# Seven products instead of eight for the last two chunks in layer 0 too, with the sums that feed them moved

## The chip, the core and the metric

The kernel runs on one NeuronCore of one Trainium2 chip. The metric is the device time of one execution in microseconds (us), lower is better. Names in the profile: PE is TensorE (matmuls), PEld its weight loads, DVE is VectorE, ACT is ScalarE, POOL is GpSimd, SP is the engine whose queue issues most DMAs. A q behind an engine's name (SPq, ACTq) is its queue issuing a DMA.

## The reference

Two layers, each an attention block and a gated MLP block, on an x of 2048 rows and 512 columns, with the same weights in both layers, all in float32:

```python
def _A_ref(x, wqkv, wo):            # linear attention, 32 heads of 16
    q, k, v = ...(x @ wqkv)
    phi = lambda t: jnp.where(t > 0, t + 1, jnp.exp(t)) + 1e-6
    kv = einsum("bhsd,bhse->bhde", phi(k), v);  z = sum of phi(k) over s
    o = (phi(q) @ kv) / (phi(q) @ z + 1e-6)
    return o.reshape(B, S, D) @ wo

def _B_ref(x, w_in, w_sp, b_sp, w_out):   # F = 1792, half of it 896
    z = _gelu(einsum("bsd,df->bsf", x, w_in))
    z1, z2 = z[..., :Fh], _layernorm(z[..., Fh:])
    g = einsum("ts,bsf->btf", w_sp, z2) + b_sp[None, :, None]
    return einsum("bsf,fd->bsd", z1 * g, w_out)

x = x + _A_ref(_layernorm(x));  x = x + _B_ref(_layernorm(x))   # twice
```

## The kernel before, in words

**Arithmetic.** Every float32 operand of a matmul is split into a high part (a copy on ScalarE, rounded to the matmul's type, `high`, L101) and a low part (the rest, a subtraction on VectorE, `low`, L104). A product is then three matmuls: high by high, high by low, low by high (`mm3`, L115 to L117). So each operand costs one ScalarE and one VectorE operation, and each 128 x 512 result over 512 columns of x costs 12 matmuls.

**Order of the work.** Nothing is scheduled by a planner: the order of the Python code is the order in which each engine gets its instructions, and each engine works through its own list in order. Waits between engines come from the tiles that they share. SBUF tiles come from lists of slots (`Slots`, L30): 22 pages of 128 x 512, 6 quads of 128 x 4 x 512, 4 larger ones; a slot that was freed first is reused first, and a DMA into it waits for its last reader.

**Stages of a layer.** x is cut into 16 tiles of 128 rows (four chunks of four tiles).

- `P1`, steps s = 1 to 17: layer norm, turning of the tile (`T`), K and Q projections, phi, and the sum G over the tiles (`Gmm(s-2)`). `start` (L416) opens it in layer 0: first loads, warm-up matmuls that compute nothing (`idle`), first tile and weights.
- `transition`: from G to the matrix that replaces attention's kv and wo.
- `P2`, steps s = 1 to 18 (`run`, L888). In step s: `c(s-1)`, attention's output of a tile, with the residual add `c2` and statistics `c_stats` (VectorE, then three small operations on GpSimd); `c3(s-1)`, normalise on ScalarE, and store the tile (yt) for turning; `b(s)` and `d(s-2)`, where a loaded tile is transposed by VectorE (L286) and split; `e(s-3)`, the half of w_in that becomes z2 (24 matmuls), with gelu `e2` and statistics `e3`; `e4(s-4)`, its normalisation; and then up to two units `f` of the other half, z1: one unit is one of 7 feature blocks of one of 4 chunks, 12 matmuls and a gelu.
- `P4`, 56 groups and then 16 tiles `o`: the spatial product with w_sp (already done with seven block products instead of eight, so it needs sums of w_sp's blocks: `Sums`, whose `tick` does two adds on GpSimd, its fetches and its stores, in P2 and P4 of layer 0), gates, and the out-projection. `join` starts the next layer's P1 beside the tiles `o`.

**Seven products.** In layer 1 alone (`self.seven`), feature blocks 0 to 5 of the chunks 2 and 3 are not computed as 12 units `f`. They are seen as a 2 x 2 block product: 3 blocks of features against 3 others, 256 columns of x against the other 256, chunk 2 against chunk 3. Seven products of 6 matmuls per block (`product`, L776) then take the place of eight. They need four sums of blocks of w_in and four sums of blocks of x:

- The weight sums are made once, by `Make` (L165): `fetch`, `add` (four operations on VectorE), `split`, `store` into a DRAM buffer, in steps beside the tiles `o` at the end of layer 0 (`make.step(i)`, L1249). In layer 1 `fetch_sum` (L769) loads them from GpSimd's queue.
- The x sums are made tile by tile of chunk 3. `whole` (L739) adds high and low part of the matching tile of chunk 2 on GpSimd, in steps 13 to 16; `block_sums` (L745) does four 256-wide subtractions on VectorE, inside `d_low` (L672); `block_parts` (L761) splits a finished half.
- The products P1 and P2 lie in the steps 14 to 16 (`side`, L861), P3 to P7 in `tail` (L821), behind step 18. The unit 6 of each chunk remains (`last_f`).

In layer 0 the units f of the chunks 2 and 3 go on until they are done, the last of them behind step 18 (`P4.run`, L1205).

Of the kernel before, what the change touches and what calls it, by code (L numbers as in the profile page):

```python
# [53 lines left out]
def mixer_kernel(ctx: ExitStack, tc: tile.TileContext, x_in, wqkv, wo_d, win1_d, win2_d, wsp_d, bsp_d, wout_d,  # L54
# [109 lines left out]

    class Make:  # L165


        def __init__(self):
            self.raw, self.sum, self.part = {}, {}, {}

        def fetch(self, g):
            self.raw[g] = load(win1_d[g]), load(win1_d[g + 3])

        def add(self, g):
            a, b = self.raw.pop(g)
            A11, A12, A21, A22 = (r.rearrange("p (c f) -> p c f", f=P)[:, s] for r in (a, b) for s in (slice(0, 2), slice(2, 4)))
            s, t = pages.get([P, 2, 2, P]), pages.get([P, 2, 2, P])
            nc.vector.tensor_add(s[:, 0], A21, A22)
            nc.vector.tensor_sub(s[:, 1], s[:, 0], A11)
            nc.vector.tensor_sub(t[:, 0], A11, A21)  # L180
            nc.vector.tensor_sub(t[:, 1], A12, s[:, 1])
            pages.put(a, b)
            self.sum[g] = s, t

        def split(self, g):
            self.part[g] = []
            for r in self.sum.pop(g):
                h, l = pages.get([P, 2, 2, P], F32R), pages.get([P, 2, 2, P], F32R)
                split(h, l, r)
                pages.put(r)  # L190
                self.part[g] += [h, l]

        def store(self, g):
            for n, p in enumerate(self.part.pop(g)):
                m = 2 * (n // 2)
                nc.sync.dma_start(kept[:, m:m + 2, g, n % 2, :], p.bitcast(F32).rearrange("p m c f -> p m (c f)"))
                pages.put(p)

        def step(self, i):
            for g in range(3):  # L200
                at = i - 2 * g
                if 0 <= at < 5:
                    (self.fetch, lambda g: None, self.add, self.split, self.store)[at](g)
# [87 lines left out]
    class P1:  # L291
# [124 lines left out]
        def start(self):  # L416
# [19 lines left out]
            idle(10)  # L436
# [3 lines left out]
            self.wk.piece()  # L440
            self.T_high(0)
            idle(4)
# [3 lines left out]
            self.wk.piece()  # L446
# [9 lines left out]
        def run(self):  # L456
# [5 lines left out]
            for s in range(1, NT + 2):  # L462
                self.loadx(s + 3)
                self.turn.load(s + 1)
                turned = 2 <= s < NT and s not in self.turn.by_pe
# [31 lines left out]
                for w in list(side)[:1 if s < 5 else 2]:  # L497
                    w.fetch()

# [69 lines left out]
    class P2:  # L569
        def __init__(self, p1):  # L570
            self.L = L = p1.L
            self.p1 = p1
            self.win1, self.win2 = w_in1(), p1.win2
            self.qturn, self.xturn = Turn(f"qt{L}", range(5), True), Turn(f"yt{L}", range(4))
            self.qp, self.qT, self.x, self.ms, self.xB, self.z, self.zms = {}, {}, {}, {}, {}, {}, {}
            self.fq = deque()
            self.fnext = []
            self.seven = self.L == 1
            self.S, self.T, self.Tp = {}, {}, {}
# [92 lines left out]
        def d_low(self, i):  # L672
            b, home, h, l = self.dpart
            low(l, b, h)
            n, k = divmod(i, 4)
            if self.seven and n == 3:
                self.block_sums(k, b)
            home.put(b)
            if i in self.xB:
                pages.put(self.xB.pop(i))  # L680
            if k == 3 and not (self.seven and n >= 2):
                self.fnext = [(n, f) for f in range(NF)]
# [30 lines left out]
        def f(self):  # L713
# [8 lines left out]
            if f == NF - 1 and not (self.seven and n == 3):  # L722
                quads.put(*self.xT.pop(n))
# [15 lines left out]
        def whole(self, k):  # L739

            h, l = (t[:, :, k * P:(k + 1) * P].bitcast(F32) for t in self.xT[2])
            self.xr = pages.get([P, 4, P])
            nc.gpsimd.tensor_tensor(self.xr, h, l, op=OP.add)

        def block_sums(self, k, y):  # L745


            p, o = divmod(k, 2)
# [4 lines left out]
            x = self.xr  # L753
# [5 lines left out]
            pages.put(x)  # L759
# [9 lines left out]
        def fetch_sum(self, m):  # L769
            self.S[m] = []  # L770
            for g in range(3):
                t = pages.get([P, 2, 2, P], F32R)
                nc.gpsimd.dma_start(t.rearrange("p i c f -> p i (c f)"), kept[:, m - 1, g])
                self.S[m].append(t)
# [27 lines left out]
        def P1(self, g):  # L802
            if g == 0:
                self.X, self.C = [], []
            self.X.append(banks.get(PAGE))
            self.product(self.X[g], "P1", g, start=True)
            self.C.append(self.copied(self.X[g]))

        def P2(self, g):
            y = banks.get(PAGE)  # L810
            self.product(y, "P2", g, start=True, stop=True)
            t = self.C[g]
# [4 lines left out]
        def last_f(self, n):  # L817
            self.fq.append((n, NF - 1))
            self.f()

        def tail(self, p4):  # L821
            self.last_f(3)
# [38 lines left out]
        def side(self, s):  # L861

            if s == 14:
                self.P1(0)
                self.P1(1)
            elif s == 15:
                self.P1(2)
                self.P2(0)
                self.fetch_sum(4)
            elif s == 16:  # L870
                self.P2(1)
                self.P2(2)
                self.fetch_sum(2)
                for m in (2, 3):
                    self.block_parts(m, 0)
            elif s == 17:
                self.last_f(2)
                self.block_parts(2, 1)
                self.block_parts(3, 1)
                self.fetch_sum(3)  # L880
            elif s == 18:
                for m in (4, 1):
                    for p in range(2):
                        self.block_parts(m, p)
            if 13 <= s < 17:
                self.whole(s - 13)

        def run(self, sums):  # L888
            w1 = self.win1
            for s in range(1, NT + 3):  # L890
# [16 lines left out]
                else:  # L907
# [32 lines left out]
                if self.seven:  # L940
                    self.side(s)
# [4 lines left out]
                if s > 7:  # L946
                    sums.tick()
                if s >= NT + 1 and not self.seven:
                    self.p4.fetch(s - NT - 1)
# [4 lines left out]
    class Sums:  # L954
# [26 lines left out]
        def tick(self):  # L981
# [3 lines left out]
            if not self.raw:  # L985
                self.fetch()
            self.fetch()
# [13 lines left out]
    class P4:  # L1001
# [189 lines left out]
        def o(self, i):  # L1191
# [6 lines left out]
            nc.vector.tensor_add(x, x, b)  # L1198
            banks.put(b)
            nc.sync.dma_start(xs[2 * self.L + 2, i], x)  # L1200
# [4 lines left out]
        def run(self, nxt):  # L1205
            p2 = self.p2
            if p2.seven:
                p2.tail(self)
            else:
                self.prepare(0, 0)  # L1210
                self.fetch(2)
                while p2.f():
                    pass
                p2.win1.free()
                self.prepare(1, 1)
                self.fetch(3)
                self.prepare(None, 2)
            self.gb = [bigs.get([P, NF, 512]) for _ in range(NCHK)]
            n = len(self.steps)
            for g in range(n):  # L1220
# [4 lines left out]
                if g in (1, 4, 7) or 8 <= g < 28:  # L1225
# [16 lines left out]
            make = Make() if nxt is not None else None  # L1242
            for i in range(NT):
                self.loadx(i + 2)
                self.gates()
                self.o(i)
                self.zsplit(i + 2)
                if make is not None:
                    make.step(i)  # L1249
# [3 lines left out]
        def join(self, i, nxt):  # L1253
# [16 lines left out]
            if i == 15:  # L1270
                nxt.T(1)

    sums = Sums()
    p1 = P1(0)
# [43 lines left out]
```

## Time and profile before

| what | value |
|---|---|
| median of 3 runs | 1393.94 us (1392.9 to 1395.38) |
| the profiled execution | 1392.76 us |
| its span, first to last instruction | 1391.0 us |
| TensorE busy | 1383.0 us, 99% of the span, 6252 instructions |
| VectorE busy | 908.8 us, 65% |
| ScalarE, GpSimd busy | 595.1 us, 43%; 429.2 us, 31% |
| DMA | 233.57 MB, mean 168 GB/s |
| P2 of layer 0, of layer 1 | about 139 to 332 us, 829 to 1016 us |
| granted TensorE clock | 1.000 over the span |

The page gives busy time per engine, the span in 40 slices, the chain of work that ended last (followed back from the last instruction to what released each step), and the costliest groups. The views of the trace give the instructions of an engine in order of time with their start, length, source line, operation and tiles; behind them in brackets stands how long the engine was idle just before, and what released it. Matmuls are pipelined: one of 128 x 512 lasts 0.39 us in the record, but the next starts about 0.23 us later, and this distance is what it costs.

### The profile page before, as it was taken

How to read it: one execution, taken by the hardware profiler on the slowest of the kernel's cores; microseconds unless marked ns; L12 is line 12 of the kernel's file. 1: busy time of each engine (PE TensorE's matmuls, PEld its weight loads, DVE VectorE, ACT ScalarE, POOL GpSimd, SP SyncE). 2: the span in 40 equal slices, each digit the busy share in tenths (PEclk: the TensorE clock that was granted, in tenths of full speed). 3: DMA queues.
4: the chain of work that ended last, by engine and by line, in shares of the span. 5: the costliest groups of instructions: out<-in, count | busy, mean ns of one | idle time of the engine just before them, and what ended most of it. 6: DMA issues, size and time to landing. Idle time of an engine off the chain costs nothing.

```text
span 1391.0 us, 17707 instructions
## 1 busy us (share of the span) xinstructions
PE 1383.0 (99%) x6252; PEld 1159.9 (83%) x6252; DVE 908.8 (65%) x1305; ACT 595.1 (43%) x922; POOL 429.2 (31%) x518
## 2 busy tenths in 40 slices
PE   9999999999999999999999999999999999999998
PEld 7888888888888888888888888888878888888887
DVE  6785777853755587666667767876666345776642
ACT  6674543444442234241366755444454432342410
POOL 3343344544135541431023424432320001123310
PEclk9999999999999999999999999999999999999999
DMA  5541256766678864357745313555454323434442
GB/s 174 171 132 59 91 167 224 260 228 211 212 246 287 297 228 137 122 203 241 266 130 177 112 45 122 174 175 173 124 187 152 106 91 129 174 129 159 167 145 90
DMA packets 148313, 233.57 MB, mean 168 GB/s; under 512 B 12416, under 2 KB 54144, under 8 KB 148224
## 3 DMA queue, kind: packets, MB, share of 16 engines
q1 hardware_dynamic: 144768, 226.15, 49.0%
q0 software_dynamic: 1728, 3.15, 0.8%
q10 hardware_dynamic: 1728, 3.15, 0.6%
q8 instruction: 49, 0.80, 0.2%
q14 instruction: 40, 0.33, 0.1%
HBM read 161.35 MB, written 71.04 MB: 167 GB/s over the span
## 4 chain that ended last, share of the span: by engine, by line
PE 96%; DVE 2%; ACT 1%; POOL 1%; issue 1%; ACTq 0%; POOLq 0%
PE bank L117 18%; PE bank L116 18%; PE bank L115 18%; PE bank L1105 13%; PE bank L1104 13%; PE bank L1103 13%; PE bank L247 1%; PE bank L793 0%; PE bank L792 0%; PE bank L791 0%; DVE st L222 0%; PE bank L434 0%; ACT qd L101 0%; ACT pg L235 0%; DVE pg L286 0%
## 5 line engine op out<-in xcount | busy, mean ns | idle before, releaser
L1104 PE MATMUL bank<-qd,pg 128*128 128x512 f32 x800 | 311.2, 389 | 0.0
L1105 PE MATMUL bank<-qd,pg 128*128 128x512 f32 x800 | 311.2, 389 | 0.0
L1103 PE MATMUL bank<-qd,pg 128*128 128x512 f32 x800 | 311.2, 389 | 0.0
L1069 DVE TENSOR_TENSOR qd<-qd,qd 128x1024 fp32r<-128x1024 f32 x112 | 158.4, 1414 | 138.7 <-ACT qd L1062 138.5
L1062 ACT ACTIVATE qd<-qd 128x1024 fp32r<-128x1024 f32 x112 | 118.6, 1059 | 235.9 <-DMA qd<-s 96.5
L1125 POOL TENSOR_TENSOR bg<-bg,pg 128x512 f32<-128x512 f32 x56 | 78.2, 1399 | 327.6 <-DMA pg<-z 302.9
L1104 PEld LDWEIGHTS bank<-qd,pg 128*128 128x128 f32 x800 | 150.2, 188 | 31.4
L1103 PEld LDWEIGHTS bank<-qd,pg 128*128 128x128 f32 x800 | 150.2, 188 | 31.3
L1105 PEld LDWEIGHTS bank<-qd,pg 128*128 128x128 f32 x800 | 150.2, 188 | 30.8
L117 PE MATMUL bank<-qd,pg 128*128 128x512 f32 x384 | 149.9, 390 | 0.0
L226 POOL TENSOR_SCALAR rs<-mv 128x1 f32<-128x1 f32 x96 | 38.5, 401 | 333.5 <-DVE mv L224 320.3
L978 POOL TENSOR_TENSOR pg<-pg,pg 128x512 f32<-128x512 f32 x64 | 93.7, 1464 | 93.8 <-DMA pg<-in_wsp_dram 85.4
L235 ACT ACTIVATE pg<-pg,nb,rs 128x512 f32<-128x512 f32 x63 | 51.1, 811 | 161.8 <-POOL nb L229 155.6
L115 PE MATMUL bank<-qd,pg 128*128 128x512 f32 x288 | 112.3, 390 | 0.0
L116 PE MATMUL bank<-qd,pg 128*128 128x512 f32 x288 | 112.2, 390 | 0.0
L115 PE MATMUL bank<-bg,qd 128*128 128x448 f32 x256 | 94.2, 368 | 1.6 <-ACT qd L101 1.6
L117 PE MATMUL bank<-bg,qd 128*128 128x448 f32 x256 | 93.6, 366 | 0.1
L116 PE MATMUL bank<-bg,qd 128*128 128x448 f32 x256 | 93.6, 366 | 0.0
L101 ACT ACTIVATE pg<-pg 128x512 fp32r<-128x512 f32 (+1 forms) x83 | 51.0, 616 | 96.5 <-DVE pg L286 51.9
L115 PE MATMUL bank<-wo,qd 128*128 128x512 f32 x224 | 87.1, 389 | 0.0
L116 PE MATMUL bank<-wo,qd 128*128 128x512 f32 x224 | 87.1, 389 | 0.0
L117 PE MATMUL bank<-wo,qd 128*128 128x512 f32 x224 | 87.1, 389 | 0.0
(156 smaller groups left out, 2689.7 us busy)
## 6 DMA issues: line engine op xcount, KB each, us to landing
qd<-s SPq DMA_DIRECT2D x64, 512.0 KB, 3.4
qd<-in_wsp_dram SPq DMA_DIRECT2D x48, 512.0 KB, 4.2
pg<-in_wsp_dram SPq DMA_DIRECT2D x64, 256.0 KB, 5.0
s<-pg SPq DMA_DIRECT2D x64, 256.0 KB, 4.8
pg<-x SPq DMA_DIRECT2D x64, 256.0 KB, 3.3
pg<-z SPq DMA_DIRECT2D x56, 256.0 KB, 3.7
x<-pg SPq DMA_DIRECT2D x48, 256.0 KB, 2.6
z<-pg SPq DMA_DIRECT2D x44, 256.0 KB, 2.9
```

The costliest lines, as they stand in the source:

```text
L101: nc.scalar.activation(h, src, AF.Copy)
L115: nc.tensor.matmul(out, ah, bh, start=start, stop=False)
L116: nc.tensor.matmul(out, ah, bl, start=False, stop=False)
L117: nc.tensor.matmul(out, al, bh, start=False, stop=stop)
L235: nc.scalar.activation(y, x, AF.Identity, bias=nb, scale=rs)
L978: nc.gpsimd.tensor_tensor(t, a, b, op=OP.add)
L1062: nc.scalar.activation(w[:, 0], r, AF.Copy)
L1069: nc.vector.tensor_sub(w[:, 1], r, w[:, 0].bitcast(F32))
L1103: m(out, h[:, o], w[:, 0, j, :], start=start, stop=False, skip_group_check=True)
L1104: m(out, h[:, o], w[:, 1, j, :], start=False, stop=False, skip_group_check=True)
L1105: m(out, l[:, o], w[:, 0, j, :], start=False, stop=stop, skip_group_check=True)
L1125: nc.gpsimd.tensor_tensor(u, u, z1, op=OP.mult)
```

## The change

1. **Seven products in layer 0 too.** `self.seven` goes; both layers take the `side` and `tail` of before's layer 1, so layer 0 loses 12 units f and gains 21 products (7 for each of 3 pairs of feature blocks).
2. **Weight sums earlier.** `Make` works in place on the loaded pages, split after split, by a written plan in steps 15 to 17 of P1 and 1 to 6 of P2 of layer 0.
3. **Block sums.** `whole` goes: VectorE adds high and low part itself. `block_sums` runs one step after its tile, in step s >= 15 behind `d`, ahead of `e4` and `e`; `block_parts` of forms 2 and 3 follow it in the steps 17 and 18, those of 4 and 1 come at the end of step 18. P1 and P2 are dealt out as one, two, two and one per step over the steps 14 to 17, and each fetch of weight sums comes a step later for form 4.
4. **Sums of w_sp.** Fetch a step ahead; in the steps 14 to 17 the tick stands ahead of the block sums; in P4 ticks at groups 1, 3, 5, 7 instead of 1, 4, 7.
5. **Start:** 8 and 2 warm-up matmuls instead of 10 and 4, the second weight piece ahead of the first tile's high part.
6. **Ends:** T(1) of the next layer ahead of o(15); the last output tile is added and stored in two halves from two queues.

In the lists of instructions TensorE has 6230 instead of 6252, VectorE 1350 instead of 1305, ScalarE 960 instead of 930, GpSimd 526 instead of 518 and SP 740 instead of 752 (DMA issues counted).

```diff
+        PLAN = {("P1", 15, 1): ("f0",), ("P1", 16, 0): ("a0", "s0"), ("P1", 16, 1): ("f1",), ("P1", 17, 0): ("s0", "a1"),
+                ("P2", 1, 1): ("s1",), ("P2", 2, 1): ("s1", "f2"), ("P2", 4, 1): ("a2",), ("P2", 5, 1): ("s2",),
+                ("P2", 6, 1): ("s2",)}
+        def step(self, *at):
+            if at[2] == 0 or at[0] == "P2":
+                self.store()
+            for what in self.PLAN.get(at, ()):
+                {"f": self.fetch, "a": self.add, "s": self.split}[what[0]](int(what[1]))
...
-            idle(10)
+            idle(8)
             self.ln_a(0)
             self.ln_a(1)
             self.ln_b(0)
             self.wk.piece()
+            self.wk.piece()
             self.T_high(0)
-            idle(4)
+            idle(2)
...
             self.T_low(0)
-            self.wk.piece()
             self.ln_b(1)
...
-            if self.seven and n == 3:
-                self.block_sums(k, b)
-            home.put(b)
+            if n == 3:
+                self.held.append((k, b))
+            else:
+                home.put(b)
...
-        def whole(self, k):
...
+        def block_sums(self):
+            k, y = self.held.popleft()
+            x = pages.get([P, 4, P])
             h, l = (t[:, :, k * P:(k + 1) * P].bitcast(F32) for t in self.xT[2])
-            nc.gpsimd.tensor_tensor(self.xr, h, l, op=OP.add)
+            nc.vector.tensor_add(x, h, l)
...
         def side(self, s):
+            if 15 <= s < 18:
+                self.P2(s - 15)
+            if 14 <= s < 17:
+                self.P1(s - 14)
+            if s == 16:
                 self.fetch_sum(4)
+            elif s == 17:
+                self.fq.append((2, NF - 1))
+                self.f()
                 self.fetch_sum(2)
+            elif s == 18:
+                quads.put(*self.xT.pop(2))
+                for m, p in ((4, 0), (4, 1), (1, 0), (1, 1)):
+                    self.block_parts(m, p)
                 self.fetch_sum(3)
...
                         self.d_low(s - 2)
+                if 14 <= s < NT + 2:
+                    sums.tick(s <= NT)
+                if s >= 15:
+                    self.block_sums()
+                if s > NT:
+                    for m in (2, 3):
+                        self.block_parts(m, s - NT - 1)
                 if s >= 4:
                     self.e4(s - 4)
                 self.xturn.load(s - 1)
...
+            if self.L == 1 and i == NT - 1:
+                for issue, s in ((nc.sync, slice(0, 256)), (nc.scalar, slice(256, 512))):
+                    nc.vector.tensor_add(x[:, s], x[:, s], b[:, s])
+                    issue.dma_start(out[:, s], x[:, s])
...
-                if g in (1, 4, 7) or 8 <= g < 28:
+                if g == 0:
+                    self.sums.fetch()
+                if g in (1, 3, 5, 7) or 8 <= g < 28:
                     self.sums.tick()
...
+                if i == NT - 1 and nxt is not None:
+                    nxt.T(1)
                 self.o(i)
```

More of the change, by code (lines that the diff above doesn't have):

```diff
@@ L193, in store @@
[L193 to L203, printed above, removed]
+            A11, A12, A21, A22 = (r[:, s] for r in self.raw[g] for s in (slice(0, 256), slice(256, 512)))
@@ L498, in run @@
                     w.fetch()
+                if self.L == 0:
+                    make.step("P1", s, 1)
     def transition(p1, p2):
@@ L939, in run @@
                 self.f()
-                if self.seven:
-                    self.side(s)
+                self.side(s)
+                if self.L == 0:
+                    make.step("P2", s, 1)
                 self.fq.extend(self.fnext)
@@ L945, in run @@
                 w1.fetch()
-                if s > 7:
+                if s == 7:
+                    sums.fetch()
+                if 7 < s < 14:
                     sums.tick()
-                if s >= NT + 1 and not self.seven:
-                    self.p4.fetch(s - NT - 1)
+                if s == NT + 2:
+                    sums.store()
             self.e4(NT - 1)
@@ L1206, in run @@
             p2 = self.p2
[L1207 to L1217, printed above, removed]
+            p2.tail(self)
             self.gb = [bigs.get([P, NF, 512]) for _ in range(NCHK)]
```

105 lines of the change are left out of this document (39 added, 66 removed).

## The prediction

> **What bounds the kernel now.** I read the page first, then the chain of work that ended last, then TensorE's own waits, then the timelines of the stretches that the change touches.
>
> ```profile
> span 1391.0 us, 17707 instructions
> PE 1383.0 (99%) x6252; PEld 1159.9 (83%) x6252; DVE 908.8 (65%) x1305; ACT 595.1 (43%) x922; POOL 429.2 (31%) x518
> ...
> PE 96%; DVE 2%; ACT 1%; POOL 1%; issue 1%; ACTq 0%; POOLq 0%
> ```
>
> TensorE is busy from end to end and carries 96% of the chain, so a matmul less is time less, unless something else becomes late. The view of TensorE's waits says how little is left to remove besides work:
>
> ```profile
> PE bank L434 <- DVE pg L429: 2.3, 1, 2.3
> PE bank L115 <- ACT qd L101: 1.6, 1, 1.6
> ```
>
> The first is the start. The second is one stall in all of layer 1. The timelines of VectorE and TensorE show it (start, length, engine, line, operation):
>
> ```profile
> 1006.23 2.22 DVE L104 TENSOR_TENSOR qd<-pg,qd 128x512 fp32r<-128x512 f32 x2 [2.17 <-ACT qd L101]
> 1008.38 1.06 DVE L286 STREAM_TRANSPOSE pg<-pg 128x512 f32<-128x512 f32 x1
> 1010.14 0.69 DVE L104 TENSOR_TENSOR qd<-pg,qd 128x512 fp32r<-128x512 f32 x1 [0.69 <-ACT qd L101]
> ```
> ```profile
> 1008.13 0.39 PE L117 MATMUL bank<-qd,bg 128*128 128x512 f32 x1
> 1010.16 0.47 PE L115 MATMUL bank<-bg,qd 128*128 128x448 f32 x1 [1.64 <-ACT qd L101]
> 1010.47 0.37 PE L116 MATMUL bank<-bg,qd 128*128 128x448 f32 x1
> 1010.88 0.47 PE L117 MATMUL bank<-bg,qd 128*128 128x448 f32 x1
> ```
>
> The x2 at 1006.23 is block_parts(2, 0) and (3, 0), issued at the end of step 16. Behind them in VectorE's queue stands the transpose of tile 15 (1008.38), and e(15) waits for what follows from it. VectorE is thus the engine that can become late, and the whole case is where its queue has room.
>
> **The sum, part by part.** TensorE's pitch: in layer 0 the 24 matmuls of two f units run from 287.50 to 292.97 us, 0.228 us each.
>
> *Seven products in layer 0.* Twelve f units of 12 matmuls go (144); 21 products of 6 come (126). 18 x 0.228 = **-4.1 us**, all on the path. The added evacuations (9 copies of 0.60 on ScalarE, 12 adds of 0.69 on VectorE) lie beside the products, as in layer 1, where no product between 1018.29 and 1038.69 us waits.
>
> *Layer 1, tile 15.* The parts of forms 2 and 3 now come after d_low(15), whole() leaves GpSimd, fetch_sum(4) comes a step later, behind c_stats(15). I walk step 16 on: P1(2) is now the last product of step 16, and step 17 has e(14) 4.9, P2(2) 1.4 and an f unit 2.7, some 9 us, while d(15) needs ScalarE's gelu, DMA issue and copy (0.63 + 0.33 + 0.60) and then 1.1 + 0.6 + 0.7. It is done some 4.5 us ahead of e(15). So the stall goes: 2.03 at 1008.13 against a pitch of 0.23, 1.8, and e(15) itself lasted 5.37 against 4.86 of other e's, 0.5: **-2.3** (ends 0 and -2.3). What is late next there is e(14): its low part comes some 2 us ahead.
>
> *Start.* Four warm-up matmuls go. The first eight end at 5.89 instead of 6.76, tile 0 is normalised at 6.02, so the transposes start about 6.05 instead of 6.60. The second weight piece moves into ScalarE's idle 0.94 us before 7.24. First matmul of K(0) at about 7.4 instead of 7.95; the pieces behind it follow 0.6 to 0.7 sooner. But the q weights' low parts stand behind statistics of a tile whose load lands at 12.44, and that does not move, so no more than that is won: **-0.65** (ends 0 and -1.3, the four matmuls' own time, 2 x 0.43 + 2 x 0.23).
>
> *T(1) of the next layer ahead of o(15).* K(1) of layer 1 shows steps of 0.38 and 0.34 us at 701.74 and 702.11 against 0.227, because the transpose of tile 1 (699.59) stands behind o(15)'s add. **-0.27** (ends 0 and -0.27).
>
> *Weight sums in the first half (Make).* Before, they lay in the last part of layer 0, where VectorE is half idle. At steps 16 and 17 of P1 they fit: VectorE idles 3.36 us ahead of 119.67 and again ahead of 125.11, and the loads (into pages that Gmm(12) and Gmm(13) free at 110.0 and 115.5) land before. The two loads for P2 go out some 3 us later on SP; tile 0 of them is used at 147. In P2 it is tight. Step 5 of layer 0 on VectorE:
>
> ```profile
> 177.43 1.07 DVE L286 STREAM_TRANSPOSE pg<-pg 128x512 f32<-128x512 f32 x1
> 178.34 0.63 DVE L602 TENSOR_REDUCE den<-pg 128x32 f32<-128x512 f32 x1
> 179.00 1.13 DVE L603 TENSOR_TENSOR den<-den,zeps 128x32 f32<-128x32 f32 x1
> 180.16 0.35 DVE L604 RECIPROCAL den<-den 128x32 f32<-128x32 f32 x1
> 180.44 0.63 DVE L104 TENSOR_TENSOR pg<-pg,pg 128x512 fp32r<-128x512 f32 x1
> ```
>
> The last row is b_low(5), done at 181.07; c(5) began at 180.92 and its third matmul, which reads that tile, started at 181.39. Cover: 0.3 us. Now add(2) at the end of step 4 puts four 256-wide operations ahead of the first row: 1.47 us by the pitch of L755 to L758 (978.05 to 979.52). The splits at steps 1 and 2 put 0.69 on VectorE and 0.63 on ScalarE ahead of c(2) (cover 0.46) and again ahead of step 3, and that chain (statistics, GpSimd, ScalarE, gelu, statistics) has no slack until step 6, when two f units give 5.5 us. Against this, the 1.13 of L603 is 0.19 when GpSimd is quiet, and it then would be. Walked through: 0.2 at c(2), some 1.1 at c(5), 0.2 at e(3): **+1.5** (ends 0.2 and 3.2; the upper one is 1.47 + 2 x 0.69 + 0.9 for one meeting with GpSimd, less the cover, and rounded up to take in ScalarE). I take the walk, between the two.
>
> *Layer 0, steps 14 to 18.* The nearest rows are layer 1's, which cost 2.3 there before the reordering, and nothing with it; layer 0 has GpSimd's adds of Sums besides, moved ahead of the block sums:
>
> ```profile
> 284.54 3.00 POOL L978 TENSOR_TENSOR pg<-pg,pg 128x512 f32<-128x512 f32 x2
> ...
> 284.89 1.49 DVE L104 TENSOR_TENSOR pg<-pg,pg 128x512 fp32r<-128x512 f32 x1 [0.75 <-ACT pg L101]
> ```
>
> That L104 takes 0.69 with GpSimd quiet (960.75), here 1.49. VectorE's step in layer 1 was 11.0 us with a b (973.01 to 984.02); add 0.69 for the sum that whole() made, and up to 2.6 for two adds, against steps of 9.0, 10.3, 10.3 and 9.0 on TensorE. e(14) has some 2 us of cover, of which 0.5 to 1.8 stay. On SP the tick's two stores and up to three loads, 0.45 us of issue each, now stand ahead of the load of yt(s-1); they lie beside the 2.3 us in which that tile's own store lands, and tile 14's load has some 2.7 us to spare behind them. fetch_sum's three issues (1.85 us on GpSimd) come behind c_stats. **+0.2** (ends 0 and 2.3).
>
> *Layer 0, the start of P4.* The tail now runs up to it, as in layer 1. There the weights of group 2 were done at 1049.53 (L1069, 1048.31 + 1.22) and group 2 begins at 1049.61, reading them 0.23 later: 0.3 us of cover. In layer 0 the first tick of Sums has loads issued as group 0 begins, and its two adds fall just there; one meeting costs 0.8. **+0.6** (ends 0 and 1.3).
>
> *The last tile in halves.* Two 256-wide adds (0.42 each) for one of 0.69, then half the bytes on a queue of its own; the write took 2.06 from issue (1387.80 to 1389.86). I take 0 (ends -0.3 and +0.3). The 4 sums of h and l in layer 1 lie under e's 4.9 us.
>
> Sum: -4.1 - 2.3 - 0.65 - 0.27 + 1.5 + 0.2 + 0.6 = **-5.0 us**. The profiled execution took 1392.76 (its span and 1.76 around it), 1.2 less than the median of 1393.94; I apply the difference to the median: **1388.9**.
>
> **Rivals.**
>
> *The stall at tile 15 stays* (the change does not do that part): for it, the row names ScalarE, whose queue in step 17 is as full as before; against it, 9 us of matmuls in front. 1388.9 + 2.3 = 1391.2.
>
> *The clock stays low longer.* The warm-up matmuls start 0.43 us apart until 5.89, and 0.23 from 6.96 on; eight of them end before that turn. If the turn comes later, K(0)'s six matmuls and its transposes up to about 9.5 us run at the low clock: 6 x 0.43 + 0.44 = 3.0 us against the 2.2 from 7.95 to 10.13, and the 0.65 is lost as well: 1388.9 + 0.65 + 0.8 = 1390.4. The Trainium skill, TensorE: Matmul & The Clock Gate, section The HAM clock gate, says that the clock is released after a window of about 3.4 us of sustained activity, which runs free of the kernel; the turn here, about 4 us after the first matmul at 2.32, agrees. By that rule the shorter run may miss one window.
>
> *VectorE becomes the bound in steps 15 to 17 of layer 0.* Price: if each of the seven operations of a step that read two SBUF tiles (two low parts, the sum of h and l, four block sums) takes 1.56 instead of 0.69, a step is 11.7 + 6.1 = 17.8 against 10.3; over steps 15 and 16, and about half of that in 17 without c, less 4 to 9 us of cover, some 9 us: 1397.9, slower. It decides once VectorE's step passes 13 us. Against it: GpSimd has two adds of 1.3 per step, so the rows bound the delay at 2.6. The Trainium skill, SBUF — State Buffer, section SBUF: two separate sides, says that VectorE with two SBUF inputs and GpSimd lock each other out for a whole instruction; the 1.49 above, ending 0.54 after the first add, agrees, and by it the delay cannot pass the adds' own time.
>
> **How the numbers follow.** Forecast 0.66, stall stays 0.10, clock 0.16, VectorE 0.08. The range goes from 1385.9 (all costs at their low ends and the start at its best: -4.1 - 2.3 - 1.3 - 0.27 + 0.2 - 0.3 = -8.1) to 1392.7 (the costs of early P2 and of steps 14 to 18 at their high ends: -7.3 + 3.2 + 2.3 + 0.6 = -1.2). It takes in the first three cases and leaves out the last, and more than two bad ends at once. 0.2% is 2.8 us, about what a measurement here can tell from no change: the bound is 1391.15. Forecast: 0.62 below it and 0.04 above; stall: 0.02 and 0.08; clock: 0.13 and 0.03. Faster 0.77, same 0.15, slower 0.08.
>
> **What would show it.** TensorE's instructions fall by 22. The wait L115 at 1010 is gone from TensorE's waits. New short waits stand at c(2), c(5) and e(3) of layer 0 (near 155, 181 and 185 us) and at the third group of its P4; no wait stands in layer 0's products. A wait of over 3 us in layer 0's steps 14 to 18 would make me wrong, as would early waits over 3 us together.

## The result, and the profile after

| | before | after |
|---|---|---|
| median of 6 executions | 1393.16 us (1392.75 to 1395.38) | 1401.23 us (1396.57 to 1403.16) |
| the profiled execution | 1392.76 us, span 1391.0 | 1396.57 us, span 1394.8 |
| granted clock of the executions | 1.000 in the profiled one | 1.000, 0.999, 0.999, 0.996, 0.996, 0.996 |

The ratio is 1.005 (95% interval 1.0039 to 1.0061): the change makes the kernel **slower by 8 us**, where 5 us less was forecast. Two parts of it must be kept apart. In the profiled execution, at a clock of 1.000, 3.8 us are added. The other executions lose 2.4 to 6.6 us more, with a lower granted clock.

From the page after:

```profile
span 1394.8 us, 17776 instructions
PE 1381.8 (99%) x6230; PEld 1155.2 (83%) x6230; DVE 936.0 (67%) x1350; ACT 604.9 (43%) x939; POOL 433.9 (31%) x526
...
PE 84%; DVE 7%; ACT 3%; issue 2%; POOL 2%; DMA 1%; ACTq 0%; SPq 0%; DVEq 0%; POOLq 0%
```

TensorE has the 22 matmuls less and 1.2 us less busy time, but its share of the chain falls from 96 to 84%: other engines now end last in places. TensorE's waits (engine and line, what it waited for: total, times, longest) name them:

```profile
PE bank L1105 <- DVE qd L1070: 2.7, 1, 2.7
PE bank L438 <- DVE pg L433: 2.3, 1, 2.3
PE bank L797 <- DMA pg<-win_sums: 1.3, 3, 0.7
PE bank L115 <- ACT pg L101: 0.9, 2, 0.5
PE bank L117 <- DVE qd L104: 0.7, 1, 0.7
PE bank L524 <- POOL pg L109: 0.4, 1, 0.4
...
```

Three rows of 0.2 or 0.3 follow. Only the second row was there before (the start). The L115 of 1.6 in layer 1 is gone, as forecast, and layer 1 has no wait left; all new ones but the start's (0.4 of the fourth row) lie in layer 0's later stages. A wait costs more than its idle time, since the matmuls right behind it come slower. I sum what each start-to-start step of TensorE of 0.28 us and more exceeds 0.227, by stretch, after less before. The start's row alone is the shift of one matmul of step 1 (17.91 us instead of 17.43), since the number of warm-up matmuls differs:

| stretch of after (us) | what | us more |
|---|---|---|
| to 18 | start | +0.5 |
| 120 to 140 | transition to P2 | +0.6 |
| 140 to 215 | P2 of layer 0, c(2), c(5), e(3) | +2.1 |
| 300 to 322 | e(14) at 314 | +1.0 |
| 322 to 346 | products P3, P6, P7 of layer 0 | +2.5 |
| 346 to 372 | third group of layer 0's P4 | +3.5 |
| 372 to 1040 | layer 1 | -2.4 |

With -4.1 for the 18 matmuls and -0.3 behind the last matmul, the sum is +3.4; measured are +3.8. Steps under 0.28 are not in the sum, and where the other 0.4 lie stays open.

**Where layer 0 and layer 1 differ.** VectorE in the steps 16 and 17 of layer 0, then in step 16 of layer 1, and below it what GpSimd does in layer 0, with its last row from layer 1 (start, length, engine, line):

```profile
312.76 1.77 DVE L104 TENSOR_TENSOR qd<-pg,qd 128x512 fp32r<-128x512 f32 x1 [1.69 <-ACT qd L101]
...
320.92 2.27 DVE L104 TENSOR_TENSOR qd<-pg,qd 128x512 fp32r<-128x512 f32 x1 [1.20 <-ACT qd L101]
323.11 1.77 DVE L754 TENSOR_TENSOR pg<-qd,qd 128x512 f32<-128x512 f32 x1
...
1002.91 0.69 DVE L104 TENSOR_TENSOR qd<-pg,qd 128x512 fp32r<-128x512 f32 x1 [1.82 <-ACT qd L101]
```
```profile
311.31 2.67 POOL L980 TENSOR_TENSOR pg<-pg,pg 128x512 f32<-128x512 f32 x2
...
321.32 3.02 POOL L980 TENSOR_TENSOR pg<-pg,pg 128x512 f32<-128x512 f32 x2
...
330.65 1.72 POOL L779 DMA_DIRECT2D pg<-win_sums  x3 [0.20 <-issue]
...
1017.82 1.70 POOL L779 DMA_DIRECT2D pg<-win_sums  x3
```

The same subtraction takes 1.77 us beside GpSimd's two adds, and 0.69 alone. The next step's takes 2.27, and the sum of h and l behind it 1.77 against 0.68. So the statistics of tile 14 come late, GpSimd's work on them too, and behind that stand the three loads of weight sums: they leave at 330.65, and P3 begins at 330.85. In layer 1 they leave at 1017.82, 4.6 us ahead of P3. These are the sums for P6; those for P7 follow them, and that is the wait L797. Of the 2.5 us in the table 0.5 are another one, of P3's third product for a gelu of ScalarE (L709).

**P4's start.** ScalarE's list in layer 0:

```profile
359.06 0.63 ACT L742 ACTIVATE pg<-pg 128x512 f32<-128x512 f32 x1 [0.40 <-ACT pg L742]
361.78 0.33 ACTq L744 DMA_DIRECT2D z<-pg  x1
362.15 0.63 ACT L742 ACTIVATE pg<-pg 128x512 f32<-128x512 f32 x1 [2.45 <-DMA z<-pg]
362.81 0.77 ACTq L744 DMA_DIRECT2D z<-pg  x1
363.68 0.63 ACT L1068 ACTIVATE pg<-pg 128x512 fp32r<-128x512 f32 x1 [0.90 <-ACT pg L742]
```

The fifth gelu is done at 359.69, but its store is issued at 361.78. In the trace a wait for semaphore 108 stands just ahead of this issue, and 108 is the semaphore on which the first of the six stores counts its end; that store lands at 361.70. The sixth gelu starts only then, at 362.15, and its store goes out as soon as it is done: that the second store lands at the same time, 362.81, is chance, for the wait ahead of the sixth issue is for another semaphore and lets it through at once. ScalarE works in order, so the operands of the next groups (L1068, L1063) stand still behind the fifth store. The view of the stores' line, in layer 0 and in layer 1, shows how much later they land (min, median, max from issue to landing):

```profile
DMA to landing us min/median/max: 2.2/5.8/6.7
```
```profile
DMA to landing us min/median/max: 2.2/3.1/4.4
```

In layer 0 the three 256 KB loads for the first tick of Sums are under way beside them, and in 360 to 368 us the DMA engines are busy without a break (share 1.00).

### The profile page after: what moved, and what is told of

Its sections match the earlier page's. It is cut to its first block, busy times and chain, and to the rows that moved or that the text cites. A ratio compares the mean times of both kernels' runs of the same rounds, so it can differ in the third digit from the quotient of the medians.

```text
span 1394.8 us, 17776 instructions
## 1 busy us (share of the span) xinstructions
PE 1381.8 (99%) x6230; PEld 1155.2 (83%) x6230; DVE 936.0 (67%) x1350; ACT 604.9 (43%) x939; POOL 433.9 (31%) x526
## 4 chain that ended last, share of the span: by engine, by line
PE 84%; DVE 7%; ACT 3%; issue 2%; POOL 2%; DMA 1%; ACTq 0%; SPq 0%; DVEq 0%; POOLq 0%
PE bank L117 15%; PE bank L116 14%; PE bank L115 14%; PE bank L1105 13%; PE bank L1104 13%; PE bank L1106 13%; DVE st L226 1%; DVE pg L104 1%; PE bank L797 1%; PE bank L799 1%; PE bank L798 1%; DVE qd L104 1%; ACT z_z L239 1%; POOL rs L231 1%; ACT qd L101 1%
## 5 line engine op out<-in xcount | busy, mean ns | idle before, releaser
L1070 DVE TENSOR_TENSOR qd<-qd,qd 128x1024 fp32r<-128x1024 f32 x112 | 162.3, 1449 | 131.3 <-ACT qd L1063 130.8
L1063 ACT ACTIVATE qd<-qd 128x1024 fp32r<-128x1024 f32 x112 | 118.7, 1059 | 238.4 <-DMA qd<-s 103.8
L1105 PEld LDWEIGHTS bank<-qd,pg 128*128 128x128 f32 x800 | 150.1, 188 | 34.0 <-DVE qd L1070 3.0
L1104 PEld LDWEIGHTS bank<-qd,pg 128*128 128x128 f32 x800 | 150.1, 188 | 31.8 <-ACT qd L1063 0.7
L1106 PEld LDWEIGHTS bank<-qd,pg 128*128 128x128 f32 x800 | 150.2, 188 | 31.4
L115 PE MATMUL bank<-qd,pg 128*128 128x512 f32 x288 | 112.5, 391 | 0.9 <-ACT pg L101 0.9
L115 PE MATMUL bank<-bg,qd 128*128 128x448 f32 x256 | 94.1, 368 | 0.0
L115 PE MATMUL bank<-wo,qd 128*128 128x512 f32 x224 | 87.1, 389 | 0.0
L117 PEld LDWEIGHTS bank<-qd,pg 128*128 128x128 f32 x384 | 72.1, 188 | 16.5 <-DVE pg L104 1.7
```

The source lines that it names most:

```text
L115: nc.tensor.matmul(out, ah, bh, start=start, stop=False)
L117: nc.tensor.matmul(out, al, bh, start=False, stop=stop)
L1063: nc.scalar.activation(w[:, 0], r, AF.Copy)
L1070: nc.vector.tensor_sub(w[:, 1], r, w[:, 0].bitcast(F32))
L1104: m(out, h[:, o], w[:, 0, j, :], start=start, stop=False, skip_group_check=True)
L1105: m(out, h[:, o], w[:, 1, j, :], start=False, stop=False, skip_group_check=True)
```

## The experiments

Spans are those of the profiled executions; the changed kernel's is 1394.8. Where the clock is at a half in a profile, that is said.

### e1: P4 of layer 0 without Sums until group 4

```diff
-                if g == 0:
+                if g == 3:
                     self.sums.fetch()
-                if g in (1, 3, 5, 7) or 8 <= g < 28:
+                if 4 <= g < 28:
```

> Layer 0's P4 leaves the sums of w_sp alone until group 4. In the changed kernel the sixth and fifth z1 store of the tail wait on ScalarE's queue until the first two stores have landed, 6.1 and 6.2 us after their issue, and the operands of group 2 stand behind them (ScalarE's L1068 9.7 us after P4's first matmul, against 7.1 in layer 1). Theory A, the three loads of the first tick beside them make the stores slow: the stores land in 2 to 4 us, L1068 stands 7.1 us after P4's first matmul, TensorE's wait of 2.7 us at L1105 falls below 0.5, span 1394.8 - 3.4 = 1391.4. Rival B, the tail's own order (six gelus and stores ahead of the operands) makes them late: the wait stays above 2 us and the span at 1394.8. On the granted clock: if the pause of TensorE at this place is what lowers it in some executions (0.996 to 0.999), all executions show 1.000 here; if the shorter warm-up at the start does, they do not.

Measured: span 1391.5; L1068 at 7.8 us after P4's first matmul (353.4); the four stores ahead of the fifth land in 2.4 to 4.0 us. The median of 11 is 1395.03, ratio 1.0016 (1.0007 to 1.0024).

```profile
PE bank L797 <- DMA pg<-win_sums: 1.4, 1, 1.4
...
PE bank L1105 <- DVE qd L1070: 0.4, 1, 0.4
```

Theory A holds: without Sums the stores land in time and ScalarE waits for none. The edit takes away the three loads and the first adds together, so it does not say which of them costs how much. Nine executions show 1.000, one 0.999, but one 0.996 (1400.72): P4's pause is not the only cause of the low clock.

### e2: the four ticks of steps 14 to 17 in steps 8 to 11

```diff
-                if 14 <= s < NT + 2:
-                    sums.tick(s <= NT)
+                if 8 <= s < 12:
+                    sums.tick()
+                if s == 14:
+                    sums.store()
...
                 if 7 < s < 14:
-                    sums.tick()
-                if s == NT + 2:
-                    sums.store()
+                    sums.tick(s < 13)
```

> The four ticks of the sums of w_sp that stood in steps 14 to 17 of layer 0 come in the middle of steps 8 to 11. Theory A, GpSimd's adds stretch VectorE's low parts (1.77 and 2.27 us where layer 1 has 0.69) and sums (1.77 against 0.68), and this delays e(14), the statistics of tile 14, GpSimd's issue behind them and the weight sums: the wait at 314 us (0.73) goes, the loads for P6 leave over 3 us ahead of P3 instead of 0.2, and the waits for win_sums (1.3 in three) go; with the slow matmuls around them 1.0 + 2.6 = 3.6 us less, span 1391.2. Rival B, the weight sums are late because their pages are late or GpSimd's queue is slow whatever else runs: the waits for win_sums stay, span 1394 or above. Third, steps 8 to 11 now have the collisions: new waits there, up to 4 x 0.7 us, span 1391 to 1394.

Measured: span 1397.7, with one window at half clock behind P4's pause (1.7 us); median of 6 1402.43, ratio 1.0070 (1.0048 to 1.0092). The waits for win_sums are gone (322 to 346: 0 instead of 2.5). But in their place stand:

```profile
PE bank L115 <- ACT qd L101: 2.1, 3, 0.9
PE bank L117 <- DVE qd L104: 1.0, 3, 0.3
```

Those at 237, 250 and 264 us are the ticks' own, 0.5 each; those at 288, 298 and 317 come when e(11), e(12) and e(14) get their tiles late. So A is right on where the waits for win_sums came from, and the third outcome, sized too small, on what follows: **the steps 8 to 11 have no free place for these adds either**, although two units f stand in them. They have a tick of their own already; other steps were not tried.

### e3 and e6: the weight sums later in P2

```diff
-                ("P2", 1, 1): ("s1",), ("P2", 2, 1): ("s1", "f2"), ("P2", 4, 1): ("a2",), ("P2", 5, 1): ("s2",),
-                ("P2", 6, 1): ("s2",)}
+                ("P2", 7, 1): ("s1",), ("P2", 8, 1): ("s1", "f2"), ("P2", 10, 1): ("a2",), ("P2", 11, 1): ("s2",),
+                ("P2", 12, 1): ("s2",)}
```

> The weight sums' splits and adds that stood in steps 1 to 6 of layer 0's P2 stand in steps 7 to 12, where two units f per step give VectorE room. Theory A, those operations delay c(2), c(5) and e(3) by some 2.0 us together: the waits at 157, 183 and 200 us go, no new one comes, span 1392.8. Rival B, the waits there come from something else of the change (pages handed out in another order, loads of P2 leaving 3 us later): they stay, span 1394.8. Pages are held longer in steps 2 to 8, so a new wait for a page there would also keep the span near 1394.8.

Measured: span 1400.7, one window at half clock at 288 us in it, behind a pause of TensorE of 2.00; median of 6 1406.65, ratio 1.0096 (1.0079 to 1.0113). 140 to 215 us has no wait left, so the early waits were these operations. But VectorE's transposes now wait for stores whose pages they take over:

```profile
DVE pg L290 <- DMA z<-pg: 6.8, 3, 2.5
...
DVE pg L290 <- DMA win_sums<-pg: 2.7, 1, 2.7
```

In the steps 14 to 18 8.2 us are lost (the window at half clock among it) instead of 1.0: the third outcome, a lack of pages, far beyond the gain.

```diff
-                ("P2", 1, 1): ("s1",), ("P2", 2, 1): ("s1", "f2"), ("P2", 4, 1): ("a2",), ("P2", 5, 1): ("s2",),
-                ("P2", 6, 1): ("s2",)}
+                ("P2", 1, 1): ("s1",), ("P2", 2, 1): ("s1",), ("P2", 4, 1): ("f2",), ("P2", 6, 1): ("a2",),
+                ("P2", 7, 1): ("s2",), ("P2", 8, 1): ("s2",)}
```

> Of the weight sums only the third third moves, two steps later: fetch in step 4, adds in step 6, splits in steps 7 and 8 of layer 0's P2. Pages are held no longer than before it. Theory A, the adds at the end of step 4 alone make c(5) late: the two waits at 183 us (1.3 with the slow matmuls) and the short one at 200 go, the one at 157 (0.3) stays: span 1394.8 - 1.6 = 1393.2. Rival B, pages: as in the run with all of it in steps 7 to 12, VectorE's transposes wait for stores whose pages they reuse, and new waits come: span 1395 or above.

Measured: span 1395.1, median of 4 1401.13, ratio 1.0059 (1.0044 to 1.0073). The losses at 183 fall from 1.3 to 0.3 and that at 200 goes, as A says; the stretch of 300 to 322 us loses 2.0 more than in the changed kernel, and P4's start 1.3 less. By itself it brings nothing.

### e4: the start as before

```diff
-            idle(8)
+            idle(10)
...
             self.wk.piece()
-            self.wk.piece()
             self.T_high(0)
-            idle(2)
+            idle(4)
...
             self.T_low(0)
+            self.wk.piece()
             self.ln_b(1)
```

> The start as before the change: 10 and 4 warm-up matmuls, the second weight piece behind the first tile's operands. Theory A, the piece ahead of the tile's high part made ScalarE late (first matmul of K(0) at 8.41 us against 7.95): it is at 7.95 again and the span 1394.3. Rival B, the shorter warm-up itself moved it, as the rise of the clock came 1.9 us later (8.33 against 6.42 us): the same time, but then the clock rises near 6.4 again and K(0) runs fast at once. If the shorter warm-up is what lowers the clock in some executions, all show 1.000 here and the median of the executions falls to some 1394 to 1397; if not, they show 0.996 to 0.999 again and it stays at 1400.

Measured: median of 5 1399.49, ratio 1.0038 (1.0026 to 1.0050), clocks 1.000 to 0.998, none at 0.996. K(0) begins at 8.58 and the clock rises at 7.67, so neither A nor B comes out. One and the same matmul of step 1 stands at 18.05 us (after: 17.91; before: 17.43). Over the profiles in which the clock does not fall back early on, it comes at 17.3 to 18.1 with 8 and 2 warm-up matmuls (mean of 9: 17.7) and at 17.4 to 18.1 with 10 and 4 (mean of 5: 17.9): **the start gains 0.2 at most**, and differences of 0.5 are chance. In this profile TensorE's pause at P4 lasts 3.8 us, and then the clock stands at a half for 6.83 us (stretches: length, busy times, granted clock, DMA share, GB/s):

```profile
366.00:369.40 3.40, 0.51 (x1) 0.19 (x1) 3.37 (x5) 0.22 (x2) 1.85 (x2) 1.00 0.81 275
369.50:376.30 6.80, 5.75 (x14) 4.54 (x15) 6.73 (x11) 3.91 (x5) 0.00 (x0) 0.50 0.01 2
376.40:380.00 3.60, 3.60 (x18) 2.93 (x17) 3.57 (x7) 2.11 (x3) 0.00 (x0) 1.00 0.05 5
```

A pause of 2.66 in the changed kernel's profile had no such end; in e2 one of 2.6 had 3.41 us of half clock behind it. The Trainium skill, TensorE: Matmul & The Clock Gate, section The HAM clock gate, says that the clock is lowered after an idle window of about 3.4 us that runs free of the kernel; the stretches of 3.41 and 6.83 agree with windows of that length, and the cases of 2.6 (e2) and 2.00 (e3) show that a pause shorter than one can be enough.

### e5: all of Sums that met the tail, in P4

In e1's kernel, the four ticks go as second ticks into the groups 8, 10, 12 and 14.

```diff
-                if 14 <= s < NT + 2:
-                    sums.tick(s <= NT)
+                if s == 14:
+                    sums.store()
...
+                if g in (2, 3):
+                    self.sums.fetch()
+                if 4 <= g < 28:
+                    self.sums.tick()
+                if g in (8, 10, 12, 14):
                     self.sums.tick()
```

> The four ticks of the sums of w_sp of steps 14 to 17 of layer 0 go into P4, as second ticks of its groups 8, 10, 12 and 14, and P4's first tick stands in group 4 as in the run with P4's start left alone (span 1391.5). Theory A, the adds collide with VectorE in the steps 14 to 18, whose TensorE work shrank because the products P3 to P7 lie behind step 18: with no add there, the low parts take 0.69 us, the wait at 313 us (0.7) goes, the weight sums leave GpSimd before P3 and no product waits for win_sums (2.0 us with the slow matmuls); P4 has room for the adds: span 1391.5 - 1.0 - 2.6 = 1388 (1387.5 to 1389). Rival B, the adds cost the same wherever they stand (moving them to steps 8 to 11 only moved the waits): new waits in P4's groups 8 to 15, span 1391 or above. All executions should show a clock of 1.000, since no pause of TensorE over 1 us is left.

Measured: span 1389.0, though the transition lost 1.3 more than in the changed kernel; median of 12 1391.30, ratio 0.9995 (0.9983 to 1.0007). From 215 to 346 us no step of TensorE is longer than its pitch, and VectorE's row of step 16 is back:

```profile
313.03 0.69 DVE L104 TENSOR_TENSOR qd<-pg,qd 128x512 fp32r<-128x512 f32 x1 [1.82 <-ACT qd L101]
```

Theory A holds: with Sums out of the way, 1.0 + 2.5 + 3.3 us of the time lost in layer 0 are gone. What it said on the clock fails: of 12 executions seven took 1389.3 to 1391.5, five 1395.3 to 1397.1 at 0.996, with no long pause left.

### e7: e5 and e6 together

The diffs of e5 and of e6, nothing else.

> The two edits before together. If their effects add: span 1388 - 1.6 = 1386.4, median of the executions near 1388.5, faster than the kernel before (1393.1) by 0.3%. If pages or the clock interfere: 1389 or above.

Measured: span 1388.2; eight of 12 executions 1389.6 to 1393.7, four 1395.8 to 1397.3 at 0.996; median 1392.53, ratio 0.9996 (0.9984 to 1.0008). The effects add in part, and the clock takes it back. e6's part also brings a loss back: in the profiles of e9, e12, e13 and e14 below, which hold both edits, one step of a product at 340 us takes 0.5 to 0.9 instead of 0.23, with no add of Sums near it; in e5 none does.

### e8: layer 1's part alone, on the kernel before

The edit is part 3 of the change, taken only where `self.seven` holds, and T(1). From its diff:

```diff
+                if self.seven and s >= 15:
+                    self.block_sums()
+                if self.seven and s > NT:
+                    for m in (2, 3):
+                        self.block_parts(m, s - NT - 1)
                 if s >= 4:
                     self.e4(s - 4)
...
+                if i == NT - 1 and nxt is not None:
+                    nxt.T(1)
                 self.o(i)
```

> The kernel before with the new order of block sums, products and fetches in layer 1, and T(1) ahead of the last tile, and nothing else of the change: layer 0 stays with eight products. Theory A, this part of the prediction was right: the wait of 1.64 at 1010 us goes, span 1391.0 - 2.3 - 0.3 = 1388.4, median 1390.5. Rival B, layer 1's gain in the changed kernel came from something else (pages, the place of the sums): the wait stays, span 1391.

Measured: 1390.67, median of 11 (1389.98 to 1391.27), all at 1.000; ratio **0.9977 (0.9969 to 0.9986)**. One wait is left, the start's:

```profile
PE bank L434 <- DVE pg L429: 2.3, 1, 2.3
```

Theory A: this part brings 2.4 us. The span, 1389.2, holds a start that came 0.5 late.

### e9 to e15: what lowers the clock

e9 is e7 with the start of before (the diff of e4), e10 is e8 with the start of the change (the same diff the other way), e11 is e8 with 4 and 0 warm-up matmuls:

```diff
-            idle(10)
+            idle(4)
...
             self.T_high(0)
-            idle(4)
```

> The kernel with both edits (sums of w_sp in P4, third third of the weight sums later), with the start as before the change (10 and 4 warm-up matmuls, old order of pieces). Its executions fell into two groups, 1389.6 to 1391.9 at a clock of 1.000 and 1395.8 to 1397.3 at 0.996, though no pause of TensorE over 0.7 us is left. Theory C, the second group comes from the shorter warm-up: here all executions show 1.000 and lie between 1389 and 1392, median 1390. Rival D, it comes from the work of layer 0 (short waits that add up): 3 or 4 in 10 executions still show 0.996.

> The kernel before with layer 1's new order (all executions 1390.0 to 1391.3 at 1.000), with the change's start: 8 and 2 warm-up matmuls, the second piece earlier. Theory C: some 3 to 5 in 10 executions show 0.996 and take 1395 to 1397. Rival D: all show 1.000, 1390 to 1391.3. The start's own time, when the clock stays at 1.000: 0 (between -0.5 and +0.5).

> The same with 4 warm-up matmuls at the start and none behind the transposes, all else as before the change. Theory C, doubled: more than half of the executions show 0.996 or less and take over 1395, and if the profiled one is among them the record of the clock shows where it stands at a half (Theory C: within the first 25 us). Rival D: 1.000 throughout, and only the first 10 us are slower, by 1 to 2 us.

Measured: e9 1389.26 (1388.51 to 1390.57, 6 executions, all at 1.000), ratio **0.9972 (0.9961 to 0.9984)**, the best of all kernels. e10 1390.54, e11 1391.92, both with none of 11 at 0.996. So neither theory stands as it was written: the start matters in e9 and not in e10. The next four, on one chip, vary only e7's start: e15 leaves it as it is, e12 takes the two `idle` lines of e4's diff (10 and 4), e13 its two lines of pieces alone (8 and 2, old order), e14 those and 4 and 0 warm-up matmuls, as e11.

> The kernel with both edits and the change's start, unaltered, as the control of this series on this chip: profiled span 1388 to 1389, and 4 in 10 executions at a clock of 0.996 and 1395 to 1397, if the second group belongs to the kernel. If none shows 0.996, the group belongs to the chip or the moment, and the runs beside it say nothing on the start.

> The control with 10 and 4 warm-up matmuls, the change's order of pieces kept. If the number of warm-up matmuls makes the second group: no execution at 0.996, all between 1388.5 and 1391.5. If the order of pieces makes it: 4 in 10 as in the control.

> The control with the old order of pieces, 8 and 2 warm-up matmuls kept. The other half: 4 in 10 at 0.996 if the number of warm-up matmuls makes the group, none if the order of pieces does.

> The control with the old order of pieces, 4 warm-up matmuls and none behind the transposes: the suspected cause doubled. If the warm-up makes the group: more than half at 0.996 or below. If not: as the control or better, and 1 to 2 us slower at the start alone, as in layer 1's kernel with few warm-ups.

| kernel | warm-up | pieces | at 0.995 or 0.996 | median |
|---|---|---|---|---|
| e15, and e7 before | 8 and 2 | new | 3 of 12, 4 of 12 | 1392.2, 1392.53 |
| e13 | 8 and 2 | old | 4 of 12 | 1391.51 |
| e12 | 10 and 4 | new | 0 of 8 | 1389.76 |
| e9 | 10 and 4 | old | 0 of 6 | 1389.26 |
| e14 | 4 and 0 | old | 0 of 11 | 1391.57 |

In this kernel the group goes with the number of warm-up matmuls, not with the order of the pieces; but fewer still do not make it worse. The start of e14 is later, though: the matmul of step 1 stands at 19.29. e15's profile shows how that can be, with a clock that rises at 5.47 us and falls again:

```profile
6.54 0.71 PE L438 MATMUL bank<-pg,ones 128*128 128x512 f32 x2
8.59 0.56 PE L115 MATMUL bank<-qd,pg 128*128 128x512 f32 x1 [1.34 <-ACT pg L101]
```
```profile
5.50:8.80 3.30, 1.71 (x9) 0.90 (x8) 1.91 (x4) 2.01 (x4) 1.58 (x4) 1.00 1.02 359
8.90:12.20 3.30, 3.30 (x11) 2.28 (x10) 1.77 (x3) 1.38 (x3) 0.00 (x0) 0.50 1.05 394
```

Two warm-up matmuls at full clock are over at 7.25, K(0) comes at 8.59, and TensorE was busy in 1.71 of 3.30 us; the clock goes back for one window. With four of them less is left of the gap: 0.63 in e12, with TensorE busy in 2.79 of the 3.41 us behind the rise, and 0.52 in e9 with 2.89. With 4 and 0 the clock first rises at 12.7, when the gap is past. But it is a close thing: in e5's profile TensorE is busy in 1.89 of the 3.41 us behind the rise, in e15's in 1.82, and e5's clock does not fall. This execution (0.999) lost one window. The group at 0.996 lost about three (0.004 x 1390 / 0.5 = 11 us at a half, some 5.5 us of time, which is what it takes more); no profile caught one, so that these windows too lie at the start is **inferred from the edits that remove them, not seen**. Why of the kernels with the same start e10 has none in 11 and e1 one in 11, but e5 five in 12, stays open.

## Why the prediction was wrong, point by point

From -5.0 to the +3.8 of the profiled execution is 8.8 us. Products and P4's start, the two steps in bold below, make 2.5 and 2.9 of it; the executions at a lower clock come on top.

- *Seven products, -4.1*: right in count. With layer 0's own waits taken off one by one, e9 is still only 1.4 us better than e8, and its layer 0 keeps 2.6 us of waits that e8 lacks: 4.1 less 2.6 is 1.5.
- *Layer 1, -2.3, and T(1), -0.27*: right, mechanism and size (e8: -2.4).
- *Start, -0.65*: wrong. Next to nothing is gained, and of the rival "the clock stays low longer" only the place was right. Rises of the clock anywhere from 5.2 to 8.5 us go with the matmul of step 1 at 17.3 to 18.1. What e15's profile shows instead is an early rise that is lost again over the gap behind the warm-up. The group at 0.996 costs 5 to 6 us in a third of the executions of e7, e13 and e15, where I wrote 0.8 and the lost 0.65; that it has this cause is inferred.
- *Early P2, +1.5*: right in mechanism and place (c(2), c(5), e(3)), measured 2.1. Not foreseen: the four adds of step 17 stand ahead of the sum of the transition (L513), and its low part on GpSimd makes TensorE wait at 130 us, +0.6.
- *Steps 14 to 18, +0.2*: mis-sized. e(14) had less cover than I gave it. "One meeting costs 0.8" was read off one row (1.49); the runs show 1.1 and 1.6 for a low part and 1.1 more for the sum behind it. The third rival named this mechanism (VectorE held up by GpSimd's adds), with a chance of 0.08, but put some 9 us into the steps 15 to 17, where 1.0 is lost (and its own terms, 7.5 twice and half of that once, less 4 to 9, give 10 to 15). That the kernel came out slower does not make that rival right.
- **The step that failed first** is the claim "no wait stands in layer 0's products", and with it "beside the products, as in layer 1", a term of 0. I checked that VectorE's delay leaves e(14) in time, but not what else stands behind it: statistics, GpSimd's queue, the loads of weight sums, and then P6 and P7: +2.5.
- **The second step that failed** is *P4's start, +0.6 (0 to 1.3)*: measured 3.5. I priced the tick's adds against VectorE and not its loads against the six stores on ScalarE's queue. By the rows the adds cost about 1 (L1074 took 1.67 instead of 0.69) and the fifth store's 2.1 us the most of the rest; e1 shows the sum of both alone (3.5 falls to 0.6).
- *Last tile in halves, 0*: the time behind the last matmul fell by 0.3, at the end of my bounds.

Both are one error of method: I carried layer 1's cover over to layer 0. The change moves 15 of 21 products behind step 18, so layer 0's last steps of P2 lose the two f units that stood beside the adds of Sums, while the adds stay. Before, the same adds in the same steps cost nothing. That the lost units alone make the difference is not shown: the tick also stands earlier in the step than before, VectorE has the sum of h and l besides, and no run separates these. The Trainium skill, SBUF — State Buffer, section SBUF: two separate sides, which I used against the third rival (a VectorE instruction with two SBUF inputs and GpSimd lock each other out for a whole instruction), agrees with the rows in size: the subtraction at 320.92 and the sum behind it took 1.58 and 1.09 us longer, 2.7 together, beside two adds that lasted 3.02. It does not in order, if the record of GpSimd's starts is exact: the Trainium skill, same section, gives the port to the instruction that starts first, and this subtraction starts 0.40 ahead of the first add. VectorE's delay thus stayed near the bound of 2.6; I was wrong to bound the delay of the whole by it, because what stood behind had no slack left.

## What to carry to other kernels

Work taken off the bounding engine is also cover taken from the others: list what ran beside it, and walk each of those queues to its last reader. Transfers in a busy stretch cost here not where they landed but where an in-order engine had to wait for an older one before it could issue the next. Look at the gap between the warm-up and the first dense matmuls before shortening the warm-up: four matmuls less gained 0.2 us at most, and this kernel then had a third of its executions 5 to 6 us slower, and none with them.

## What the runs showed of the hardware

- A store issue on ScalarE's queue stood 2.1 us, until an older store had landed, and held the engine's computations up with it.
- Half clock came in pieces of 3.41 us: one behind pauses of TensorE of 1.34 (e15, in a start half idle), 2.00 (e3) and 2.6 us (e2), two behind one of 3.8 us (e4), none behind one of 2.66 us (the changed kernel).
- A 128 x 512 subtraction of VectorE took up to 2.27 us beside GpSimd's adds, against 0.69 in layer 1 with GpSimd quiet.
